# Retention and ELU layer on one core: the second chunk earlier in the opening, and the small weights of two Strassen products moved from GpSimd to VectorE

## Chip, core and metric

The kernel runs on one core of a Trainium2 chip. The metric is the device time of one execution in microseconds. The kernel before takes 636.76 us (median of 3 runs, 635.6 to 637.08). The profiled execution of it has a span of 634.4 us. All data is fp32.

## What is computed

A recurrent retention layer (4 batches, 8 heads, 768 tokens, head size 64) feeds a two-layer network with an ELU between its layers (3072 tokens, width 512, inner width 2048):

```python
for t in range(S):
    state = gamma * state + outer(k[:, :, t], v[:, :, t])
    y[:, :, t] = scale * q[:, :, t] @ state
x = y.transpose(0, 2, 1, 3).reshape(B * S, H * D)       # (3072, 512)
h = x @ w_in                                            # w_in (512, 2048)
g = where(h > 0, h, exp(min(h, 0)) - 1)
out = g @ w_out                                         # w_out (2048, 512)
```

The weights arrive as 64-bit floats, two 32-bit words each, and the kernel turns them into fp32 on the chip.

## The kernel before

**Tiling.** The recurrence is done in chunks of 128 tokens (24 of them), four of which make a block of 512 tokens (6 blocks, called tb 0 to 5). A chunk gets scores (L307), a mask (L318, L328), products for the state after each half of 64 tokens (L338), sums of states (L348, L350), and outputs: products within the chunk (L394) and with earlier states (L409), multiplied by a table of powers of gamma (`etab`, made by ScalarE at L249) into x (L433 for the first two chunks, L384 after that). V is scaled first (L281), by VectorE for chunks 0 and 1 and by GpSimd for the others. Small copies named `seen` stand between two groups of matmuls into the same bank.

**The two GEMMs.** Block 0 has a plain first GEMM (`plain_first`, L489), while the weights are still being decoded. In each piece of weights ScalarE makes three parts (`prepare`, L164 to L168) and VectorE joins them (`decode`, L190 to L194); its `yield`s let the caller place the steps among other work with `take()`. Raw weights and later the small sums pass through the three buffers of the pool `stage`. Block 1 has a Strassen first GEMM with seven products of half size (`first` and `strassen`, L698 to L756, matmuls at L740). Its banks are a (two buffers), b and d (one each). From block 1 on, the second GEMM is Strassen in two levels (`second_twice`, L933): seven outer products, in the order 1, 2, 6, 7, 5, 3, 4, each with seven inner products of four 128-column matmuls at L953. An inner product's sums are L961 and L986 (ScalarE copies) and L965 (VectorE); the inputs of the next outer product are made at L827. From block 2 on, the outer products M2 and M3 of the first GEMM are done in two levels as well (`first_twice`, L865).

**Small weights.** Two-level products need sums of quarters of the weights. They are made once, sent to DRAM (`scratch2` for the second GEMM, `scratch3` for M2 and M3 of the first one), and fetched again in every block into a ring of 11 buffers `wq` (`fetch_small`, L799 and L804), one fetch for each product consumed. For M2 and M3, `combine_small(j)` makes four sums of 128x512 on GpSimd (L816) into a `stage` buffer during the first GEMM of block 1, and puts the transfer on the list `to_send`, which `send_small` issues on the queue of SyncE.

**What sets the order.** The order of every engine's work is written by hand: it is the order of calls in the program, and each engine goes through its own list in order. All DMAs are issued by SyncE, in order too, so that a transfer that waits holds those behind it. Generators are advanced with `next` at chosen places. In the second GEMM of block 1 the generator `sec` yields "first", "middle" and the product's number at each outer product. The caller counts them in `step` (step 1 is outer product 2, step 3 is product 7, step 4 is product 5, step 5 is product 3), and does the recurrence of block 2 at the visits in `VISITS`.

`unread` issues a matmul on a blank tile whose result nobody reads. `hold` copies one element on GpSimd, so that a transfer into a buffer is ordered behind other work.

Of the kernel before, what the change touches and what calls it, by code (L numbers as in the profile page):

```python
# [9 lines left out]
FP32 = mybir.dt.float32  # L10
# [8 lines left out]
def kernel(  # L19
# [32 lines left out]
    nc = tc.nc  # L52
    PSUM = bass.MemoryType.PSUM
    P = nc.NUM_PARTITIONS

    B, H, S, D, DM, DFF = dims
    NTOK = B * S
    C = P
    TB = 512
    TH = TB // 2  # L60
# [51 lines left out]
    def hold(t, other):  # L112

        if other is not None:
            nc.gpsimd.tensor_copy(t[0:1, 0:1], other[0:1, 0:1])
# [28 lines left out]

    def prepare(parts=1, by_vector=False, between=None):

        n = len(prepared)
        if n >= NPIECE:  # L150
            return
        t = staged[n]
        if n < 2 * NQ:
            dst = (w_a, w_b)[n % 2][n // 2].rearrange("p a b c d -> p (a b c d)")
        else:

            dst = w_s[n % NQ].rearrange("p a b c d -> p (a b c d)")[:, 0:1024]
        todo = []
        for part in range(parts):
            if part and between:  # L160
                between()
            c = slice(part * 1024 // parts, (part + 1) * 1024 // parts)
            lo, hi, flat = t[:, c, 0], t[:, c, 1], dst.bitcast(U32)[:, c]
            nc.scalar.activation(flat, lo, AF.Copy, scale=2.0**-29)  # L164
            top = dst.bitcast(F8).rearrange("p (c b) -> p c b", b=4)[:, c, 3]
            nc.scalar.activation(top, hi.bitcast(FP32), AF.Copy, scale=2.0**-120, saturate=False)
            if not by_vector:
                nc.scalar.activation(lo.bitcast(FP32), hi.bitcast(FP32), AF.Copy, scale=2.0**-112)  # L168
            todo.append((lo, flat, hi if by_vector else None))
        prepared.append((dst, todo))  # L170
# [75 lines left out]
    def powers_of(tokens):  # L246
        for a in range(2):
            for u in range(2):
                nc.scalar.activation(etab[:, a, u, tokens], post[:, tokens], AF.Exp, scale=lny[:, a, u : u + 1])  # L249
# [239 lines left out]
    def plain_first():  # L489

        tiles = [(n, w, row, fi) for n in range(NQ) for w, row in ((w_a, 0), (w_b, 1)) for fi in range(2)]
        banks = []

        def part(k, columns):
            n, w, row, fi = tiles[k]
            for j in range(4):
                nc.tensor.matmul(
                    banks[k][:, columns], lhsT=w[n][:, fi, j // 2, j % 2, :], rhs=xb[:, j, columns],
                    start=(j == 0), stop=(j == 3), skip_group_check=True,
                )  # L500

        for k in range(5):
            hp = bank("aabd"[k]) if k < 4 else ps_r.tile([P, 2, TH], FP32, name="hp", tag="r")
            banks.append(hp.rearrange("p a b -> p (a b)"))
            if k == 0:
                part(0, slice(0, C))
                yield
                part(0, slice(C, 2 * C))
            else:
                part(k, half[0])  # L510
            if k:
                yield
        for k in range(5):
            part(k, half[1])
            n, w, row, fi = tiles[k]
            elu(g_plain[row * NF + 2 * n + fi], banks[k])
            yield
        for k, (n, w, row, fi) in enumerate(tiles[5:]):
            hp = bank("aabd"[k % 4]).rearrange("p a b -> p (a b)")
            for j in range(4):  # L520
                nc.tensor.matmul(  # L521
                    hp, lhsT=w[n][:, fi, j // 2, j % 2, :], rhs=xb[:, j, :], start=(j == 0), stop=(j == 3)
                )
            elu(g_plain[row * NF + 2 * n + fi], hp)
            yield
        flush()
# [114 lines left out]
    def send_small():  # L641
        while to_send:
            nc.sync.dma_start(*to_send.pop(0))
# [163 lines left out]

    W_IN = {2: w_a_[:, :, :, 1], 3: w_s_[:, :, 2]}

    def combine_small(j, behind=None):  # L810

        t = stage.tile([P, 4, 4, P], FP32, name="wi", tag="stage")
        hold(t.rearrange("p k f d -> p (k f d)"), behind)
        a11, a12, a21, a22 = (W_IN[j][:, 2 * r : 2 * r + 2, :, c, :] for r in range(2) for c in range(2))
        s1, s2, s3, s4 = (t[:, k].rearrange("p (n f) c -> p n f c", f=2) for k in range(4))
        tt = lambda o, x, y, op: nc.gpsimd.tensor_tensor(out=o, in0=x, in1=y, op=op)  # L816
        tt(s1, a21, a22, ALU.add)
        tt(s2, s1, a11, ALU.subtract)
        tt(s3, a11, a21, ALU.subtract)
        tt(s4, a12, s2, ALU.subtract)  # L820
        to_send.append((scratch3[j - 1], t.rearrange("p k f d -> p (k f d)")))

    xs = {}

# [271 lines left out]
    def take(count=1):  # L1096
        for _ in range(count):
            next(piece, None)
# [3 lines left out]
    def unread(count, n):  # L1102
        for _ in range(count):
            nc.tensor.matmul(warm[:, 0:n], lhsT=blank[:, 0:P], rhs=blank[:, 0:n], start=True, stop=True, skip_group_check=True)
# [15 lines left out]
    y = outputs_of_first()  # L1120
    next(y)
    next(y)
    unread(1, TB)
    score_products(sc, 0, 0, 1)
    state_sum(kvs, 0, 0, 0, 1)
    prepare(2, between=lambda: powers_of(slice(2 * C, S)))
    piece = decode(True)
    take()
    take()
    scale_v(1)  # L1130
    mask_pair(sc, 1)
    inner = plain_first()
    next(inner)
    state_products(kvs, 0, 0, 1, range(2))
    state_sum(kvs, 0, 0, 1, 0)
    next(y)
    next(y)
    next(y)
    unread(1, TB)
    next(y, None)  # L1140
    take()
    take()
# [2 lines left out]
    scale_v(2)  # L1145
    scale_v(3)
    prepare(2, by_vector=True)
    next(inner)
    piece = decode()
    take()  # L1150
    take()
    next(inner)
    scores(0, 1)
    states(0, 1)
# [5 lines left out]
    y = outputs(0, 1)  # L1160
# [115 lines left out]
    sides = [  # L1276
        itertools.chain(combine_w_in(1), last), itertools.chain(combine_w_in(2), combine_w_in(3)), iter(()), iter(()),
    ]
    smalls = [2], [], [3], []
    for n in range(NQ):  # L1280
        load(2 * CPB + n)
        cur = first(n)
        for at in range(3):
            next(cur)

        for _ in tail:
            pass
        for s in cur:
            next(sides[n], None)
            next(sides[n], None)  # L1290
            if s == "gap":
                break
        for _ in sides[n]:
            pass
        tail = cur
        for j in smalls[n]:
            combine_small(j, w_s[1].rearrange("p s a b c -> p (s a b c)") if j == 2 else None)
        send_small()
    for m in range(2 * CPB, 3 * CPB):
        scale_v(m)  # L1300
# [14 lines left out]
        pass  # L1315
    flush()
    step, VISITS = 0, [(0, "end"), (2, "middle"), (3, "first"), (4, "end"), (5, "end")]
    for s in sec:
        if s == "first":
            step += 1  # L1320
        at = (step, s if s in ("first", "middle") else "end")
        if at in VISITS:
            retention_step(2, VISITS.index(at))
        if s == ORDER2[-1]:
            break
    tail = sec
# [150 lines left out]
```

## Time and profile before

| part of the page | value |
|---|---|
| span | 634.4 us |
| TensorE busy | 626.7 us, 99% |
| VectorE busy | 481.7 us, 76% |
| ScalarE busy | 252.9 us, 40% |
| GpSimd busy | 40.6 us, 6% |
| DMA | 136.85 MB, mean 216 GB/s |

The page and the timeline call TensorE's matmuls PE, its weight loads PEld, VectorE DVE, ScalarE ACT, GpSimd POOL, and SyncE's queue SPq. A line of the timeline has the start in us from the span's start, the duration in us, engine, line of the program, operation, and what it writes and reads with shapes and count; in brackets stands the engine's idle time just before it, with the work whose end released it. The ends of matmuls are modelled: a group's listed duration is about 0.16 us longer than its share of TensorE, so the steps between starts are the better measure. The steps are 0.893 us for an inner product at L953, 1.73 us for a product at L740 or at L497 with 256 columns.

The opening lasts until about 30 us. The first GEMM of block 1 runs from 135 to 186 us, the second GEMM of block 1 from 182 to about 240.

### The profile page before, as it was taken

The page shows a single profiled execution, that of the slowest core. Times are in us where ns is not written, and L with a number is a line of the kernel's source. Part 1 is how long each engine was busy: PE and PEld are TensorE (multiplying, and loading weights), DVE is VectorE, ACT ScalarE, POOL GpSimd, SP SyncE. Part 2 cuts the span into 40 slices and gives each one's busy share as a digit, 9 for nine tenths or more (in the row PEclk, how much of TensorE's full clock was granted, in tenths as well). Part 3 has the DMA queues.
Part 4 walks back from the last instruction along what each step waited for, and adds up shares of the span by engine and source line. Part 5 has one row for each costly group of instructions (what it writes and reads, how often), then busy time and mean ns, then how long its engine had stood idle before and what let it go on. Part 6 is the DMA issues. An engine that isn't in the chain of part 4 may idle for free.

```text
span 634.4 us, 16149 instructions
## 1 busy us (share of the span) xinstructions
PE 626.7 (99%) x6680; PEld 560.7 (88%) x6680; DVE 481.7 (76%) x870; ACT 252.9 (40%) x472; POOL 40.6 (6%) x40
## 2 busy tenths in 40 slices
PE   8999999999999999999999999999999999999998
PEld 5764568888899999889999989999988999988997
DVE  5779979978879685589676598867489878558975
ACT  6599635014551113554112556111465311366311
POOL 1111000003600000200000100000110000000000
PEclk9999999999999999999999999999999999999999
DMA  8698867687477778504889701789820697700794
GB/s 336 264 390 307 269 205 222 189 248 258 176 239 228 242 254 272 239 2 135 277 267 312 290 4 55 258 283 286 302 100 4 218 299 236 238 24 2 231 309 158
DMA packets 75897, 136.85 MB, mean 216 GB/s; under 512 B 6320, under 2 KB 31792, under 8 KB 70704
## 3 DMA queue, kind: packets, MB, share of 16 engines
q1 hardware_dynamic: 75824, 135.82, 64.2%
q8 instruction: 53, 0.87, 0.5%
q14 instruction: 20, 0.16, 0.1%
HBM read 114.56 MB, written 21.23 MB: 214 GB/s over the span
## 4 chain that ended last, share of the span: by engine, by line
PE 94%; DVE 4%; issue 1%; ACT 0%; DVEq 0%
PE pa L953 20%; PE pa L911 10%; PE pd L953 10%; PE pb L953 5%; PE pa L865 5%; PE pb L911 4%; PE pa L521 3%; PE qa L911 3%; PE x L611 3%; PE pa L740 2%; PE pd L865 2%; PE qd L911 2%; PE pd L911 2%; PE pa L611 2%; PE y L394 2%; PE kv L338 2%
## 5 line engine op out<-in xcount | busy, mean ns | idle before, releaser
L961 ACT COPY ms<-pa 128x128 f32<-128x128 f32 x104 | 27.6, 265 | 147.1 <-PE pa L953 143.7
L953 PE MATMUL pa<-ts,wq 128*128 128x128 f32 x560 | 74.2, 275 | 0.0
L953 PE MATMUL pd<-ts,wq 128*128 128x128 f32 x552 | 73.6, 276 | 0.1
L953 PEld LDWEIGHTS pa<-ts,wq 128*128 128x128 f32 x560 | 68.5, 192 | 0.4
L953 PEld LDWEIGHTS pd<-ts,wq 128*128 128x128 f32 x552 | 67.1, 192 | 0.9 <-DVE res L965 0.5
L953 PE MATMUL pa<-gC,wq 128*128 128x128 f32 x480 | 64.6, 278 | 0.0
L478 ACT ACTIVATE r<-r 128x512 f32<-128x512 f32 x96 | 60.5, 631 | 3.0
L953 PEld LDWEIGHTS pa<-gC,wq 128*128 128x128 f32 x480 | 59.0, 192 | 1.3
L477 ACT ACTIVATE r<-gC 128x512 f32<-128x512 f32 x64 | 39.9, 624 | 32.0 <-DVE gC L919 32.0
L965 DVE TENSOR_TENSOR res<-pd,ms 128x128 f32<-128x128 f32 x68 | 19.4, 286 | 39.6 <-PE pd L953 38.4
L281 POOL TENSOR_TENSOR chunk<-chunk,vf 128x512 f32<-128x512 f32 x22 | 26.3, 1199 | 318.4 <-DMA chunk<-in_qkv_dram 153.5
L481 DVE SCALAR_TENSOR_TENSOR gC<-r,gC 128x512 f32<-128x512 f32 x64 | 44.3, 724 | 0.7 <-ACT r L478 0.7
L827 DVE TENSOR_TENSOR ts<-gC,ts 128x512 f32<-128x512 f32 x60 | 41.3, 688 | 1.0
L827 DVE TENSOR_TENSOR ts<-gC 128x512 f32<-128x512 f32 x60 | 40.9, 682 | 0.0
L953 PE MATMUL pb<-gC,wq 128*128 128x128 f32 x240 | 31.7, 275 | 0.0
L986 ACT COPY res<-pa 128x128 f32<-128x128 f32 x34 | 9.0, 265 | 55.1 <-PE pa L953 55.1
L953 PEld LDWEIGHTS pb<-gC,wq 128*128 128x128 f32 x240 | 29.2, 192 | 0.0
L690 ACT COPY m<-pa 128x512 f32<-128x512 f32 x24 | 13.9, 581 | 30.1 <-PE pa L911 14.2
L919 DVE TENSOR_TENSOR gC<-qa,gC 128x512 f32<-128x512 f32 x8 | 5.5, 692 | 25.1 <-PE qa L911 18.3
L911 PE MATMUL pa<-xt,w_s 128*128 128x256 f32 x96 | 23.0, 382 | 0.0
L911 PE MATMUL pa<-xt,w_b 128*128 128x256 f32 x96 | 23.0, 382 | 0.0
L965 DVE TENSOR_TENSOR res<-res 128x512 f32<-128x512 f32 (+1 forms) x31 | 20.6, 666 | 3.0 <-DVE res L965 0.5
(256 smaller groups left out, 1258.4 us busy)
## 6 DMA issues: line engine op xcount, KB each, us to landing
wq<-scratch_dram SPq DMA_DIRECT2D x277, 256.0 KB, 4.2
chunk<-in_qkv_dram SPq DMA_DIRECT2D x23, 1024.0 KB, 8.3
wraw<-in_w_dram SPq DMA_DIRECT2D x15, 1024.0 KB, 6.1
out_dram<-res SPq DMA_DIRECT2D x14, 256.0 KB, 3.8
scratch_dram<-gT SPq DMA_DIRECT2D x12, 256.0 KB, 4.2
scratch_dram<-m SPq DMA_DIRECT2D x12, 192.0 KB, 5.6
scratch_dram<-so SPq DMA_DIRECT2D x4, 512.0 KB, 4.8
scratch_dram<-wi SPq DMA_DIRECT2D x2, 1024.0 KB, 5.1
```

What stands on the lines that cost most here:

```text
L281: eng.tensor_tensor(out=kv[:, 1], in0=kv[:, 1], in1=vf[:, i].unsqueeze(2).to_broadcast([C, H, D]), op=ALU.mult)
L477: nc.scalar.activation(e, h, AF.Relu, scale=-1.0)
L478: nc.scalar.activation(e, e, AF.Exp, scale=-1.0)
L481: nc.vector.scalar_tensor_tensor(g, e, -1.0, h, ALU.add, ALU.max)
L521: nc.tensor.matmul(hp, lhsT=w[n][:, fi, j // 2, j % 2, :], rhs=xb[:, j, :], start=(j == 0), stop=(j == 3))
L611: nc.tensor.matmul(X[j][:, d, :], lhsT=w[j][:, d * P : d * P + P], rhs=x[j], start=(n == 0 and d == 0), stop=at_end, skip_group_check=True,)
L827: sub = lambda o, x, y: nc.vector.tensor_tensor(out=o, in0=x, in1=y, op=ALU.subtract)
L865: nc.tensor.matmul(ps[:, f, :], lhsT=lhs[f], rhs=xs[j][k], start=(begin and f == 0), stop=True, skip_group_check=True,)
L911: nc.tensor.matmul(ps[:, fi, :], lhsT=w[:, fi, j2, :], rhs=x[:, j2, :], start=(j in (1, 7) and fi == 0 and j2 == 0), stop=(j2 == 1), skip_ ...
L953: nc.tensor.matmul(ps, lhsT=w[:, f, :], rhs=ts[j][k][:, f, :], start=(begin and f == 0), stop=(f == 3), skip_group_check=True,)
L961: nc.scalar.copy(m, ps)
L965: nc.vector.tensor_tensor(out=o, in0=x, in1=y, op=ALU.add)
```

## The change

It has two parts.

In the opening, the work of chunk 1 (scores, scaling, mask, states, outputs) goes ahead of the decode of the first weights and of the first columns of the first GEMM, which used to stand between its scores and its state products. One blank matmul becomes half as wide, and one is dropped. ScalarE makes the powers for tokens 256 and up (L249) after the weights' first two pieces, and no longer between the halves of the first. The tile k = 3 of `plain_first` is done in two halves of columns, with the scores and states of chunks 2 and 3 between them.

The eight small sums of M2 and M3 leave GpSimd and the first GEMM of block 1. VectorE makes them in the second GEMM of block 1, in four pairs, at the visits listed in `SUMS`. They go into the buffer `xt`, which lies idle there, and M2's and M3's sums use it one after the other: M3's first sum overwrites what M2's transfer reads. The transfers are issued at the end of step 3 and in the middle of step 5.

```diff
-    def prepare(parts=1, by_vector=False, between=None):
+    def prepare(parts=1, by_vector=False):
...
-            if part and between:
-                between()
...
+            elif k == 3:
+                part(k, slice(0, C))
+                yield
+                part(k, slice(C, 2 * C))
...
-    def combine_small(j, behind=None):
+    def combine_small(j):
-        t = stage.tile([P, 4, 4, P], FP32, name="wi", tag="stage")
-        hold(t.rearrange("p k f d -> p (k f d)"), behind)
+        t = xt_.rearrange("p j a (b c) -> p j (a b) c", c=P)
...
-        tt = lambda o, x, y, op: nc.gpsimd.tensor_tensor(out=o, in0=x, in1=y, op=op)
+        tt = lambda o, x, y, op: nc.vector.tensor_tensor(out=o, in0=x, in1=y, op=op)
         tt(s1, a21, a22, ALU.add)
         tt(s2, s1, a11, ALU.subtract)
+        yield
         tt(s3, a11, a21, ALU.subtract)
         tt(s4, a12, s2, ALU.subtract)
         to_send.append((scratch3[j - 1], t.rearrange("p k f d -> p (k f d)")))
+        yield
...
-    unread(1, TB)
+    unread(1, TH)
     score_products(sc, 0, 0, 1)
     state_sum(kvs, 0, 0, 0, 1)
-    prepare(2, between=lambda: powers_of(slice(2 * C, S)))
+    prepare(2)
     piece = decode(True)
-    take()
-    take()
     scale_v(1)
     mask_pair(sc, 1)
-    inner = plain_first()
-    next(inner)
     state_products(kvs, 0, 0, 1, range(2))
     state_sum(kvs, 0, 0, 1, 0)
     next(y)
+    take()
     next(y)
+    take()
     next(y)
-    unread(1, TB)
+    inner = plain_first()
+    next(inner)
     next(y, None)
...
     prepare(2, by_vector=True)
+    powers_of(slice(2 * C, S))
     next(inner)
     piece = decode()
     take()
     take()
+    next(inner)
     next(inner)
     scores(0, 1)
...
-    smalls = [2], [], [3], []
...
-        for j in smalls[n]:
-            combine_small(j, w_s[1].rearrange("p s a b c -> p (s a b c)") if j == 2 else None)
         send_small()
...
+    smalls = itertools.chain(combine_small(2), combine_small(3))
+    SUMS = [(3, "first"), (3, "middle"), (4, "end"), (5, "first")]
     for s in sec:
...
+        if at in SUMS:
+            next(smalls)
+        if at in ((3, "end"), (5, "middle")):
+            send_small()
```

## The prediction

> **What bounds the kernel now.** TensorE does. I read the page's shares first (PE 99% of a 634.4 us span), then its slices, then TensorE's own timeline, for the few places where it waits.
>
> ```profile
> PE   8999999999999999999999999999999999999998
> ...
> PEclk9999999999999999999999999999999999999999
> ```
>
> Only the first and last slices of PE fall below 9, and the granted clock is full throughout. So the change can win only what TensorE waits in two places, and can lose wherever it makes TensorE wait anew. The first place is the opening:
>
> ```profile
> 10.81 0.69 PE L307 MATMUL sc<-chunk 64*64 64x64 f32 x32
> 11.83 1.13 PE L497 MATMUL pa<-xb,w_a 128*128 128x128 f32 x8 [0.33 <-DVE w_a L194]
> 12.89 0.69 PE L338 MATMUL kv<-chunk 64*64 64x64 f32 x32
> ...
> 15.20 1.12 PE L1104 MATMUL pa<-blank 128*128 128x512 f32 x2
> 16.16 3.11 PE L497 MATMUL pa<-xb,w_a 128*128 128x128 f32 x16
> 19.79 1.99 PE L497 MATMUL pb<-xb,w_b 128*128 128x256 f32 x8 [0.52 <-DVE w_b L194]
> ```
>
> Chunk 1 has landed by 10.8, but its state products (L338) begin at 12.89, since the decode of w_a and the first GEMM columns go first. The 512-column product on blank at 15.20 is filler. The second place is the first GEMM of block 1, with PE, DVE and POOL side by side:
>
> ```profile
> 153.56 1.99 PE L740 MATMUL pd<-xb,w_s 128*128 128x256 f32 x8 [0.73 <-DVE h L695]
> ...
> 166.42 1.99 PE L740 MATMUL pd<-xb,w_s 128*128 128x256 f32 x8 [0.44 <-DVE h L695]
> ```
> ```profile
> 146.14 1.63 DVE L647 TENSOR_TENSOR wi<-w_s 128x384 f32<-128x384 f32 x1
> 147.81 1.51 DVE L647 TENSOR_TENSOR wi<-wi,w_s 128x384 f32<-128x384 f32 x1
> 149.24 0.54 DVE L647 TENSOR_TENSOR wi<-w_s 128x384 f32<-128x384 f32 x1
> ```
> ```profile
> 145.63 1.73 POOL L816 TENSOR_TENSOR wi<-w_a 128x512 f32<-128x512 f32 x1
> ```
>
> The same VectorE sum takes 0.54 us alone and 1.5 to 1.6 us beside GpSimd's; VectorE then is late with the L695 sum that frees bank d, and TensorE waits.
>
> [...] The trace agrees (0.54 against 1.63 above; the L695 sums, with one input in PSUM, stay at 0.69 beside a busy GpSimd). [...] No wait here is over 0.8 us and the clock is full[...]. [...]
>
> **Part 1, the opening.** Chunk 1's work moves ahead of the w_a decode, the columns 0:128 of tile 0 behind it; one filler is halved (its end is hidden by chunk 1's landing, cost and gain nothing), one is gone, the 2.55 us of powers (L249) move into ScalarE's idle 17.7 to 22.9 (nothing), and tile 3 is split around the scores. Walked with the durations of the timeline: V scaled 10.8 to 11.5 (0.68), masks to 12.2 (0.75), state sum 12.25 to 12.7, within-chunk products to 12.8, across-chunk to 13.4, the `seen` copies to 13.7 (the decode step is emitted behind them and ends at 14.3), remaining across-chunk to 14.2, the two outputs (L433) 14.25 to 15.0. They began at 15.34: 1.1 us earlier. Columns 0:128 then run 14.35 to 15.25 and 128:256 to 16.1. The second half of w_a needs ScalarE, which is tied to its DMA (about 12.3) and is done by 14.4; its decode runs to 16.1, tile 1 from 16.15 to 17.9. The decode of w_b's first half was L194 at 18.43, stretched to 1.31 us by GpSimd's scale of chunk 2 at 18.12 (landing-bound, stays). It now runs 17.3 to 18.0, ahead of that scale, so tile 2 starts at 18.05, not 19.79: 1.7. The second half then meets the scale, ends at about 20.2, and tile 3's first half waits 0.45 for it. Scores 21.15, states 22.15, rest of tile 3 23.2, outputs of pair 1 at 24.1 for 25.66: **1.55 us** remain. After 28.5 TensorE waits for nothing until 153, so this should reach the end. Ends: 0.6 (if bound to DMA landings) and 1.9.
>
> **Part 2, removed from GpSimd.** Eight L816 sums (1.27 to 1.73 us each) and a 1x1 copy go. From 142.30 to 157.18 TensorE needed 14.88 us for eight products of 1.73 plus one gap's worth: 8 x 1.7265 = 13.81, so 1.07 lost; from 157.18 to 170.05 seven products are 12.09 of 12.87, so 0.78 lost. Sum 1.85 us. Something comes back: the loads of chunks 9 to 11 stood behind the small sends on the queue and their scales behind the sums (POOL 168 to 176.6). Now they load at about 148.5 and are scaled at about 153 to 160, where VectorE has no idle. Each scale (1.04 us) delays a two-SBUF-input operation by about 0.6 (L481 at 175.82: 1.30 for 0.68), 1.8 in all, against about 1.6 of slack which I count ahead of the L695 sum of the second wait (VectorE's 11.2 us of work from 151.2 end at 162.4, it may end at 164.0). I take 0.2 lost: **gain 1.65**; ends 1.15 and 1.85.
>
> **Part 3, added to VectorE.** Eight 128x512 sums in pairs. A pair costs what a pair of L827 costs: 0.71 + 0.61 = 1.32. They write the idle xt tile: last read by L740 in block 1's first GEMM (186), next written by L454 at 241.67. Where they fall:
>
> ```profile
> 215.65 0.29 DVE L965 TENSOR_TENSOR res<-pd,ms 128x128 f32<-128x128 f32 x1 [0.41 <-ACT ms L961]
> ...
> 234.71 0.28 DVE L965 TENSOR_TENSOR res<-pd,ms 128x128 f32<-128x128 f32 x1
> ```
> ```profile
> 217.83 1.06 PE L953 MATMUL pd<-ts,wq 128*128 128x128 f32 x8
> ...
> 235.16 1.06 PE L953 MATMUL pd<-ts,wq 128*128 128x128 f32 x8
> ```
>
> The first two pairs stand on each side of four L827 sums, ahead of the 215.65 add. That add moves to 212.63 + 1.32 + 2.6 + 1.2 = 217.7 and ends at 218.0; the product into bank d, due at 217.83, waits for it: 0.2, with its restart 0.3. The third pair lands in VectorE's idle 1.43 before the add at 226.93: nothing, if the first send has landed (issued about 218, 5.1 us for 1 MB by the DMA list, against the pair's 224.9). The fourth pair costs in full: from 226.93 to 237.2 VectorE has no idle at all, and the add at 234.71 ends 0.17 before TensorE writes bank d at 235.16. So +1.32 there, on top of the 0.3: **cost 1.6 us**. The next block, without added sums, shows how tight that point is:
>
> ```profile
> 335.36 0.28 DVE L965 TENSOR_TENSOR res<-pd,ms 128x128 f32<-128x128 f32 x1
> ```
> ```profile
> 335.70 1.16 PE L953 MATMUL pd<-ts,wq 128*128 128x128 f32 x8
> ```
>
> There the add comes 0.80 after the start of the product before it (334.56), in block 1 only 0.44 (234.27): 0.36 later, and the chain of waits already runs through it. Ends of the cost: 0.3 and 2.6. The sends (SyncE) delay weight fetches behind them: the first by 2 us (weights come 10 us ahead, landing 4.2), the second holds the first fetch for M3 until about 237; it lands at 242, its product comes at about 248. Nothing.
>
> **Sum**: -1.55 - 1.65 + 1.6 = -1.6, so 636.76 becomes **635.1 us**.
>
> **The rivals.** *VectorE absorbs the sums* (18%): the fourth pair is made up because TensorE's finish, not VectorE, starts each run; cost 0.3, gains 1.55 + 1.85: -3.1, 633.7. For it: VectorE is only 64 to 74% busy there; against it: the 0.17. *The gains are smaller* (20%): the opening is held by landings (0.6), the chunk scales keep 0.7 of the middle waits (1.15), cost 1.6: -0.15, 636.6. For it: DMA at 0.92 to 1.03 share from 5 to 25 us. *A new wait on xt* (12%, slower): the third pair overwrites the tile that the first send still reads; with 8.3 us to landing, as 1 MB chunk loads take, the pair waits from 224.9 to 226.3, its 0.7 of slack goes and 0.7 is added, and the fifth stage starts later by a restart, 0.3: cost 2.6; with no gain in the opening and 1.15 in the middle: +1.45, 638.2. For it: VectorE is in order; against it: the 5.1 measured for sends of this size.
>
> **Numbers.** The forecast has 50%. Around it the error is some 0.6 us, so 36 of these 50 are faster by over 0.2% (1.27 us), 14 within. With the absorbing case (18) and 3 of the second rival: faster 57%, same 31%, slower 12%. The range 633.6 to 637.0 holds the absorbing case and the small-gain one and leaves out the new wait.
>
> **What would show it.** Right: outputs of pair 1 at about 24.1; no L740 wait of over 0.3 us between 140 and 170; from about 209 to 235 TensorE falls back by about 1.6, most of it at the bank-d product of the last inner stage, released by the L965 add. Wrong: that product not waiting (cost too high), a wait of L817 for a DMA on xt (the slow rival), or an opening that gains under 1 us (landings).

## The result and the profile after

The changed kernel takes **640.73 us** (median of 4 runs, 639.2 to 641.51) against 636.67 (4 runs) of the kernel before: ratio 1.006, 95% interval 1.0037 to 1.0084. The forecast was 635.1, with 637.0 as the upper end of its range: it has the wrong sign, and none of its rivals reaches so high. The profiled executions span 639.0 us (after) and 634.4 us (before), a difference of 4.5 us.

First the page of the kernel after, part 2, the slices of TensorE and of its granted clock:

```profile
PE   7899999999999989999999999999999999999998
...
PEclk9999999999999999999999999999999999999999
```

Two slices more than before have fallen below 9: the one from 16 to 32 us, in the opening, and the one from about 224 to 240 us, in the second GEMM of block 1; the first slice has gone from 8 to 7. The clock is still full. So the loss is again in places where TensorE waits, and the list of its waits names them (columns: who waits, for whom; us in total, how often, the longest):

```profile
PE pb L956 <- issue: 2.1, 1, 2.1
...
PE pd L495 <- DVE w_b L192: 1.3, 1, 1.3
PE pd L742 <- DVE h L697: 0.7, 1, 0.7
PE pd L956 <- DVE res L968: 0.7, 1, 0.7
PE kv L336 <- issue: 0.7, 1, 0.7
PE y L407 <- issue: 0.6, 1, 0.6
```

Three of the six shown are put down to "issue": the profile shows nothing that TensorE waited for. They sum to 3.4 us, and the prediction had no term for any of them.

To see where the time goes, I took the start of the first product of five stages from TensorE's timeline, for every kernel that ran, and subtracted neighbours (us). "To hp" is the opening up to the first product of the fifth tile of the first GEMM of block 0; the next columns end at the first GEMM of block 1, at its second GEMM, and at the first GEMM of block 2 (its products with 128 columns).

```
kernel                        to hp  to 1st GEMM   1st GEMM   2nd GEMM   rest   span
                                     of block 1    block 1    block 1
before                        28.50    106.90       46.74      58.32    393.98  634.4
before, profiled again        28.00    106.78       46.74      58.33    393.99  633.8
after                         29.80    107.41       45.98      62.14    393.64  639.0
e1  opening alone             29.35    106.43       46.72      59.01    394.49  636.0
e9  opening, no split         30.36    107.36       46.72      58.33    393.65  636.4
e3  after, no split           27.43    107.40       45.87      61.34    393.65  635.7
e11 after, V scaled by DVE    29.36    106.95       45.86      63.44    394.37  640.0
e2  sums alone                28.01    107.36       46.08      61.28    393.64  636.4
e5  after, no sums            29.59    106.41       45.83      59.82    393.63  635.3
e4  after, sends early        29.87    107.35       44.90      60.49    393.63  636.2
e10 after, half sends         29.31    107.14       45.84      63.78    393.58  639.6
e6  after, less filler        31.23    107.86       45.83      65.90    394.36  645.2
e7  sums in idle places       29.30    106.65       46.04      58.87    395.33  636.2
e8  all together              27.13    106.44       44.89      59.04    397.77  635.3
```

After minus before: +1.30, +0.51, -0.76, +3.82, -0.34, in all +4.53. The opening, meant to win 1.55, lost 1.3; the first GEMM of block 1 won half of what was forecast; its second GEMM, expected to give up 1.6, gave up 3.8. (The second column lies between 106.4 and 107.9. e2, whose instructions are those of before up to the end of that stretch, has 107.36, so I put the 0.5 down to neither part. The 0.34 of the last column is not explained.)

The opening on TensorE, kernel after (start, duration, line, tiles, count, and in brackets the idle time before it with its releaser):

```profile
14.84 3.77 PE L495 MATMUL pa<-xb,w_a 128*128 128x128 f32 x24 [0.23 <-ACT wraw L166]
18.62 1.97 PE L495 MATMUL pb<-xb,w_b 128*128 128x256 f32 x8
21.91 1.16 PE L495 MATMUL pd<-xb,w_b 128*128 128x128 f32 x8 [1.32 <-DVE w_b L192]
23.00 1.16 PE L305 MATMUL sc<-chunk 64*64 64x64 f32 x64
...
28.36 0.69 PE L407 MATMUL y<-chunk 64*64 64x64 f32 x31 [0.33 <-DVE seen L376]
29.66 0.21 PE L407 MATMUL y<-chunk 64*64 64x64 f32 x1 [0.61 <-issue]
29.80 1.56 PE L495 MATMUL hp<-xb,w_a 128*128 128x256 f32 x6
```

Up to tile 2 most of the forecast gain is there: tile 2 starts at 18.62, for 18.05 forecast and 19.79 before. Then tile 3's first half, now ahead of the scores, stands 1.32 us on the second half of w_b, and everything behind it in TensorE's order stands too. VectorE and GpSimd at that moment:

```profile
18.39 1.29 DVE L188 TENSOR_SCALAR wraw<-wraw 128x512 f32<-128x512 f32 x1
...
20.28 1.57 DVE L192 CUSTOM_DVE_ANT_0 w_b<-wraw,w_b 128x1024 uint16<-128x1024 uint16 x1
```
```profile
17.80 1.58 POOL L279 TENSOR_TENSOR chunk<-chunk,vf 128x512 f32<-128x512 f32 x1 [2.40 <-DVE wraw L189]
20.27 1.04 POOL L279 TENSOR_TENSOR chunk<-chunk,vf 128x512 f32<-128x512 f32 x1 [0.89 <-DMA chunk<-in_qkv_dram]
```

Not one but two steps of the decode fall beside GpSimd's scales of V: 1.29 us for a step that takes 0.42 alone, and 1.57 for one of 0.69. The decode ends at 21.85; the forecast had 20.2. (The second scale was there before as well, at 20.37, beside a decode step that began at 20.67 and took 1.31 us; the forecast counted one scale alone.)

The second GEMM of block 1, TensorE and then VectorE:

```profile
225.40 0.50 PE L956 MATMUL pb<-gC,wq 128*128 128x128 f32 x3
227.97 0.82 PE L956 MATMUL pb<-gC,wq 128*128 128x128 f32 x5 [2.07 <-issue]
...
239.93 1.16 PE L956 MATMUL pd<-ts,wq 128*128 128x128 f32 x8 [0.73 <-DVE res L968]
```
```profile
239.60 0.28 DVE L968 TENSOR_TENSOR res<-pd,ms 128x128 f32<-128x128 f32 x1
```

The wait of 0.73 is the one foreseen for the fourth pair of sums, behind the add of bank d. That of 2.07 is new: it falls in the middle of a product, between the third and the fourth of eight recorded matmuls with the same input, the same weight tile and the same bank (each matmul of the program leaves two records here: eight for the four of an inner product). The profile shows no semaphore that the fourth waited for.

**What "issue" was here.** The trace records, beside the data transfers, a queue of packets of 16,384 bytes that carry instructions:

```profile
q8 instruction: 53, 0.87, 0.5%
```

There are 53 of them in each of eight profiles (before twice, after, e6, e8 to e11), for some 13,400 recorded matmuls and weight loads of TensorE, so one for about 126 matmuls; I read them as TensorE's own instructions. One of them lies from 225.70 to 226.63; TensorE goes on at 227.97, 1.34 us after it has landed. In the kernel after, four of the 53 have a wait put down to issue of 0.2 us or more behind them (2.07, 0.70, 0.61 and 0.23 us), in the kernel before none. The theory that the experiments test is that TensorE stands when such a packet comes late; the rival is that the wait belongs to the work at that place.

### The profile page after: what moved, and what is told of

It reads as the page before. It is cut to its first block, busy times and chain, and to the rows that moved or that the text cites. A ratio compares the mean times of both kernels' runs of the same rounds, so it can differ in the third digit from the quotient of the medians.

```text
span 639.0 us, 16160 instructions
## 1 busy us (share of the span) xinstructions
PE 625.2 (98%) x6686; PEld 560.6 (88%) x6686; DVE 483.4 (76%) x878; ACT 252.8 (40%) x472; POOL 27.1 (4%) x31
## 4 chain that ended last, share of the span: by engine, by line
PE 86%; DVE 8%; issue 2%; ACT 1%; DMA 1%; SPq 0%; DVEq 0%
PE pa L956 19%; PE pa L914 10%; PE pd L956 10%; PE pb L956 5%; PE pa L868 5%; PE pb L914 4%; PE qa L914 3%; PE x L613 3%; PE pa L742 3%; PE pd L868 2%; PE qd L914 2%; PE pd L914 2%; PE pa L613 2%; PE y L392 2%; PE pd L742 2%
## 5 line engine op out<-in xcount | busy, mean ns | idle before, releaser
L956 PEld LDWEIGHTS pb<-gC,wq 128*128 128x128 f32 x240 | 29.3, 192 | 2.3 <-issue 2.3
L914 PE MATMUL pa<-xb,w_a 128*128 128x256 f32 x96 | 22.7, 379 | 0.0
```

Source lines behind the costliest of these rows:

```text
L914: nc.tensor.matmul(ps[:, fi, :], lhsT=w[:, fi, j2, :], rhs=x[:, j2, :], start=(j in (1, 7) and fi == 0 and j2 == 0), stop=(j2 == 1), skip_ ...
L956: nc.tensor.matmul(ps, lhsT=w[:, f, :], rhs=ts[j][k][:, f, :], start=(begin and f == 0), stop=(f == 3), skip_group_check=True,)
```

## The experiments

All ratios are to the kernel before, run on the same chip, with 95% intervals.

**The opening alone (e1)** and **the sums alone (e2).** Each is the kernel before with one half of the diff.

```diff
 # e1: before, with the new order of the opening and
+            elif k == 3:
+                part(k, slice(0, C))
+                yield
+                part(k, slice(C, 2 * C))
 # e2: before, with the sums of combine_small on nc.vector into xt, and
+    SUMS = [(3, "first"), (3, "middle"), (4, "end"), (5, "first")]
```

> The opening's part alone; the small sums stay on GpSimd. Theory A (the opening loses, because the first half of tile 3 now waits for w_b's decode ahead of the scores, and because TensorE sits in the middle of groups with no semaphore to wait for): the product after the first GEMM's fifth tile starts about 1.1 us later than before, the time is 1.1 to 1.9 us over before (ratio 1.002 to 1.003). Theory B (the prediction's: the opening gains and the loss is all in the second GEMM): 1.5 us under before (ratio 0.9976). The two waits of L740 for VectorE, 0.73 and 0.44 us, stay in both.

> The small sums' part alone, with the opening as before. Theory A (the send of 1 MB holds up TensorE's instruction stream, a stall of about 2 us in the middle of an inner product in the fourth or fifth outer product, beside 1.3 us of VectorE's queue and 0.8 to 1.2 us saved in the first GEMM): 2 to 2.5 us over before (ratio 1.003 to 1.004). Theory B (the sums cost only VectorE's queue): within 0.5 us of before (ratio 0.999 to 1.001), with no stall in the middle of a product.

Measured: e1 1.003 (1.0016 to 1.0045), e2 1.0022 (1.0008 to 1.0035). Each half makes the kernel slower by itself. The opening of e1 ends at 29.35, within the 29.3 to 29.9 of every kernel with the split and the full filler; e2, with the opening of before, at 28.01. What the second GEMM of block 1 loses belongs mostly to the sums' half: +2.96 in e2 (1.2 of it a wait put down to issue), +0.69 in e1.

**The sends moved (e4)** and **the sums left out (e5).** e4 is the kernel after with the two sends of xt made in the first GEMM of block 1 (they carry what xt holds then, not the sums). e5 is the kernel after with the eight additions left out; xt is sent as it is.

```diff
 # e4, in the loop of the first GEMM of block 1
+        for j in ([2], [], [3], [])[n]:
+            to_send.append((scratch3[j - 1], xt_.rearrange("p j a t -> p (j a t)")))
 # e5
-        tt(s1, a21, a22, ALU.add)
-        tt(s2, s1, a11, ALU.subtract)
...
-        tt(s3, a11, a21, ALU.subtract)
-        tt(s4, a12, s2, ALU.subtract)
```

> The changed kernel with its two 1 MB sends issued during the first GEMM of block 1, where the kernel before had them; they then carry what xt held before the sums, so the small weights of M2 and M3 are left out of the result. The sums stay where the change put them. Theory A (the send holds up TensorE's instructions or weights): the 2.07 us stall in the middle of the product into bank b is gone, and the time is about 2 us under the changed kernel (ratio to before about 1.003). Theory B (VectorE's sums hold TensorE there, by whatever path): the stall stays, ratio 1.006. The wait of the bank-d product of the last inner stage, 0.73 us in the changed kernel, stays in both and grows.

> The changed kernel with the eight sums left out, so that the two sends, in their places, carry what xt held. Theory A (stall by the send; 1.3 us by VectorE's queue, apart from each other): the stall of about 2 us in the middle of a product stays, the waits of bank-d products for L968 vanish, about 1.3 us under the changed kernel (ratio to before about 1.004). Theory B (VectorE's sums are behind all of it): no stall, about 3.4 us under the changed kernel (ratio 1.001).

Measured: e4 1.0022 (0.9999 to 1.0044), e5 1.0027 (1.0012 to 1.0043). TensorE's waits from 140 us (e4) and 183 us (e5) to 245 us:

```profile
PE pd L955 <- DVE res L967: 0.7, 1, 0.7
PE pb L955 <- issue: 0.4, 1, 0.4
```
```profile
PE pb L952 <- issue: 1.2, 1, 1.2
```

The two losses come apart. Without sends at that place the wait for instructions falls from 2.07 to 0.4 and the wait for the bank-d add stays; without sums the bank-d wait goes and 1.2 of the other stays. (That last figure is no measure of the sums' share: e2 and e3, with the same sums and sends, have 1.2 and 1.4.) e4 also shows something that I hadn't asked of it: no wait is left in the first GEMM of block 1, which takes 44.90 us, 1.84 less than before. Its sends stand ahead of the loads of chunks 9 to 11 in the queue, and the last of GpSimd's scales runs at 167.34 instead of 162.29 us.

**Less filler (e6).** 12 filler matmuls of 64x64 instead of 28: each later matmul stands 16 places earlier in the program, which is 32 recorded matmuls (6654 in all for 6686). The expectation below took 16 places of the program for 16 recorded rows.

```diff
-    for n in range(28):
+    for n in range(12):
```

> The kernel after, with 12 filler matmuls of 64x64 in the opening instead of 28, so that every later matmul stands 16 places earlier in TensorE's instruction stream. If the wait of 2.07 us in the second GEMM of block 1 is one for the next block of instructions, it stays at the same row of the stream (2377) and so falls 16 matmuls further on in the work: at 230 to 231 us, in the bank-d product L956 after the one where it was, not in the bank-b product at 227.97; its length may change, since the sends are then further behind it. If it belongs to the work (the product, its weights, the bank), it stays in the bank-b product with its 2 us. Time between 638.5 and 641 either way; the opening's waits put down to issue should move by 16 matmuls as well.

Measured: 1.0162 (1.0125 to 1.0198), far outside what I had expected. But its profile is the clearest on the cause. The opening, and the second GEMM of block 1:

```profile
13.26 0.27 PE L392 MATMUL pb<-chunk 64*64 64x64 f32 x2 [0.71 <-issue]
...
28.68 0.70 PE L392 MATMUL y<-chunk 64*64 64x64 f32 x33 [2.76 <-issue]
...
211.33 1.33 PE L336 MATMUL kv<-chunk 64*64 64x64 f32 x24 [2.89 <-issue]
...
233.22 1.06 PE L956 MATMUL pb<-gC,wq 128*128 128x128 f32 x8
```

Counting TensorE's recorded matmuls from 0, the first wait in the opening stands before row 223 in both kernels. In the kernel after that is a state product (L336), here it is an output product (L392). The wait of 2.76 stands before row 477: in e1 and e11 (below) that matmul belongs to tile 3, here to the outputs. The bank-b product that stood for 2.07 us runs through. So the waits stay with positions in the stream and not with the work: the expectation of the instruction theory. Its other half, that the wait at row 2377 moves on in the work, can't be seen here; that block was in time, and one three blocks earlier (211 us) was late. e2 and e3 show it. They have six and eight recorded matmuls fewer ahead of that place, and they wait at the same row, to within one, which now lies in the next product, the one into bank a. In e3:

```profile
223.81 0.39 PE L952 MATMUL pa<-gC,wq 128*128 128x128 f32 x2
225.56 0.83 PE L952 MATMUL pa<-gC,wq 128*128 128x128 f32 x6 [1.36 <-issue]
```

The size of e6's loss has a second part: after each of the two long waits the granted clock was down.

```profile
30.00:36.00 6.00, 5.83 (x49) 5.04 (x50) 3.04 (x7) 0.51 (x1) 0.00 (x0) 0.72 0.21 46
...
212.00:218.00 6.00, 6.00 (x39) 5.88 (x36) 1.56 (x4) 0.53 (x2) 0.00 (x0) 0.52 0.26 65
```

(Busy time of PE, PEld, DVE, ACT and POOL in each stretch, then clock, DMA share, GB/s.) Behind the waits of 2.76 and 2.89 us the mean clock was 0.72 from 30 to 36 us and 0.52 from 212 to 218; elsewhere it fell behind shorter waits (below).

**Smaller sends (e10).** The kernel after with each 1 MB send made as two of 512 KB at different times.

```diff
-        if at in ((3, "end"), (5, "middle")):
+        if at in ((3, "middle"), (4, "first"), (5, "first"), (5, "middle")):
             send_small()
```

> The kernel after, with each of the two 1 MB sends made as two of 512 KB at different times (about 217.5, 221.5, 233 and 237 us); the sums stay where they were. If the 2.07 us wait of the bank-b product at 227.97 comes from the megabyte in front of TensorE's next block of instructions, it falls below 1 us, and block 1's second GEMM loses about 2.5 us against the kernel before instead of 3.8: 639.5 us. If the size of a send does not matter, the wait stays at 1.5 to 2.1 us and the time at 640.7. The wait of 0.7 us behind the bank-d add is to stay in both.

Measured: 1.0047 (1.0033 to 1.0062). The wait is the same to the matmul:

```profile
224.50 0.50 PE L958 MATMUL pb<-gC,wq 128*128 128x128 f32 x3
227.07 0.84 PE L958 MATMUL pb<-gC,wq 128*128 128x128 f32 x5 [2.07 <-issue]
```

So my picture of one megabyte in front of the instructions was wrong: the halves, issued at 215.18 and 219.80, do as much harm. The DMA engines were no freer: share 1.05 from 220 to 222 us and 1.03 from 224 to 226, as after (1.07 and 0.99), where the kernel before had 0.84 and 0.52. (Its second GEMM takes 63.78 us, more than the 62.14 of the kernel after: from 227.8 to 231.1 its granted clock was 0.50.)

What goes with the wait in all kernels is how late the packet starts. I took the moment at which row 2250 starts (a few records are missing, so the row is good to some matmuls), one block before the wait, and the start of the next instruction packet:

```
kernel         packet starts after row 2250    wait put down to issue there
e9                       2.3 us                      0
before (twice)           2.6, 2.6                    0
e6, e7, e8               2.9, 2.9, 3.0               0
e1, e4                   3.4, 3.6                    0.5, 0.4
e3, e2, e5               4.2, 4.3, 4.4               1.4, 1.2, 1.2
e11, after, e10          5.1, 5.2, 5.2               2.0, 2.1, 2.1
```

The block's matmuls take 5.2 us when nothing stands (from 219.84 to 225.05 in the kernel before). The packet takes 0.9 (0.93 in the kernel after) and TensorE goes on about 1.3 us after it has landed (1.34), so it may start about 3 us after the row (an estimate: 5.2 less 0.9 and 1.3); each microsecond beyond has about a microsecond of waiting beside it in the table (3.4 and 0.5, 5.2 and 2.1). The six kernels at the bottom all issue a send of xt in the 5 us or so before that row. That isn't enough for a late packet, though: e6, e7 and e8 do so too and don't wait. e7 issues its halves at 215.17 and 221.43 us, 5.0 before the row and 1.3 after it, with a DMA share of 1.02 from 220 to 222 us and 1.03 from 224 to 226, and its packet is in time.

**The split of tile 3.** e3 is the kernel after with tile 3 in one piece behind scores and states; e9 is e1 without the split; e11 keeps the split, but takes away what made it wait: VectorE scales chunks 2 and 3 itself, behind the decode of w_b.

```diff
 # e3 and e9
-            elif k == 3:
-                part(k, slice(0, C))
-                yield
-                part(k, slice(C, 2 * C))
...
-    next(inner)
 # e11
-        eng = nc.vector if m < 2 else nc.gpsimd
+        eng = nc.vector if m < 4 else nc.gpsimd
...
-    scale_v(2)
-    scale_v(3)
     prepare(2, by_vector=True)
...
     take()
     take()
+    scale_v(2)
+    scale_v(3)
```

> The kernel after, with tile 3 again done in one piece behind the scores and states (its first 128 columns no longer ahead of them). If the split is what the opening loses by (tile 3's first half waits 1.32 us in TensorE's order for the second half of w_b), pair 1's scores begin at about 21.0 instead of 23.0 and the opening is 1.2 us shorter than in the kernel after: near 639.5 us, and the shift against the kernel before at 31 us is about 0. If the opening loses by TensorE's instruction blocks[...], the waits put down to issue take the place of the one that is gone and the shift at 31 us stays near +1: 640.5. Everything behind 31 us should be as in the kernel after: the 2 us wait put down to issue at row 2377 of TensorE's matmuls stays.

> The new order of the opening alone (chunk 1 first, half the filler, the powers later), without the split of tile 3; the sums on GpSimd as in the kernel before. If the split is what turned the opening's gain into a loss, the fifth tile's first product (hp) begins at about 27.4 us, as in the kernel after without the split, against 28.5 before and 29.4 to 29.9 with it: a gain of 0.5 to 1.1 us, 635.7 to 636.3 us, ratio 0.999. If the opening's time is set by when loads and instruction blocks land, which differ from run to run, hp begins anywhere between 28 and 29.5, and the ratio is 1.000 to 1.003 as with the split.

> The kernel after with the split of tile 3 kept, but the two scales of chunks 2 and 3 (1.58 and 1.04 us on GpSimd, beside the decode of w_b) done by VectorE behind that decode, so that nothing stretches it: the second half of w_b should be decoded by 20.1 us instead of 21.85, and tile 3's first half should wait under 0.3 us instead of 1.32. If the stretched decode is all that the split loses by, the fifth tile's first product (hp) begins at about 28.3 instead of 29.8, and the time falls by 1.3 to 1.5 us: ratio about 1.0035 to the kernel before for 1.006. If the split also loses by waits put down to issue that come with it (rows 477 and 605 of TensorE's matmuls in five of the six profiles with the split, none in the profiles without), these stay at 0.5 to 1.2 us each, hp begins at 29 to 29.5, and the ratio stays at 1.005 or more.

Measured: e3 1.0008 (0.9989 to 1.0028) where the kernel after has 1.006; e9 0.9989 (0.9974 to 1.0003) where e1, the same with the split, has 1.003. Both pairs say that the split costs 0.4 to 0.5%, some 2.6 to 3.3 us, and that the rest of the new opening order costs nothing or gains a little. (e9's own profile isn't a good witness of it: there a wait of 1.6 us for instructions ended at 13.28, and from 14 to 21 us the granted clock was 0.51.) One cost of the new order stays without the split: in all ten kernels that have it TensorE stood for 0.3 to 1.6 us before row 223, in the four profiles with the old order not at all. e3's opening:

```profile
20.41 1.16 PE L305 MATMUL sc<-chunk 64*64 64x64 f32 x64
21.39 1.11 PE L336 MATMUL kv<-chunk 64*64 64x64 f32 x64
22.43 1.99 PE L495 MATMUL pd<-xb,w_b 128*128 128x256 f32 x8
...
27.43 0.89 PE L495 MATMUL hp<-xb,w_a 128*128 128x256 f32 x3
```

The scores run while w_b is still being decoded, and hp comes 1.07 us earlier than before. e11 shows that the split costs more than its own wait. Its ratio is 1.0058 (1.0037 to 1.0079), no better than after, though the wait for w_b is gone:

```profile
20.14 1.05 PE L495 MATMUL pd<-xb,w_b 128*128 128x128 f32 x8
21.12 1.16 PE L305 MATMUL sc<-chunk 64*64 64x64 f32 x64
22.10 1.11 PE L336 MATMUL kv<-chunk 64*64 64x64 f32 x64
23.14 1.05 PE L495 MATMUL pd<-xb,w_b 128*128 128x128 f32 x7
25.77 0.27 PE L495 MATMUL pd<-xb,w_b 128*128 128x128 f32 x1 [1.57 <-issue]
...
29.22 0.21 PE L407 MATMUL y<-chunk 64*64 64x64 f32 x1 [0.61 <-issue]
29.36 1.99 PE L495 MATMUL hp<-xb,w_a 128*128 128x256 f32 x8
```

Scores at 21.12, states at 22.10, the rest of tile 3 at 23.14: the times of my walk (21.15, 22.15, 23.2), now that the decode ends at 19.8. And then TensorE stands, once on its last matmul of tile 3 and once on the last of the outputs, for the blocks whose packets start at 23.40 and 26.89 us. Taking one wait away, 1.32 us, brought hp forward by 0.44. In the profiles with the split, one or both of these two block ends (rows 477 and 605) stood for 0.5 to 2.8 us; in those without it there was no wait of more than 0.2 us at them. In the kernel after, 127 of the 128 recorded matmuls between the two ends are products of 64x64, which TensorE runs at about 15 ns each (64 from 21.12 to 22.10 in e11); this block took 3.45 us in most kernels with the split, which is 1.1 from its beginning to the next packet's start, 1.0 for the packet and 1.3 to go on. Tile 3 in halves has eight recorded matmuls more than in one piece, so that the block begins and ends eight places earlier in the work. In e3 the same rows hold 121 products of 64x64 and seven matmuls of hp with 256 columns (0.22 us each), which fill the time until the next block is there. That these slow matmuls are what is missed is my reading; that the waits come with the split is what the runs show.

**The sums at idle places (e7).** The opening of before; each pair of sums directly ahead of an add that waits for TensorE anyway, and each pair sent on its own.

```diff
             if j == 1:
                 yield "tail"
+            if at in (2, 3, 4, 5) and tb == 1:
+                yield "idle"
             for _ in before:
...
     for s in sec:
+        if s == "idle":
+            next(smalls)
+            continue
...
-        if at in SUMS:
-            next(smalls)
-        if at in ((3, "end"), (5, "middle")):
+        if at in ((2, "first"), (3, "middle"), (4, "middle"), (5, "middle")):
```

> The opening of the kernel before, the eight sums on VectorE as in the kernel after, but each pair at a place where VectorE waits for TensorE anyway (directly ahead of the add that reads bank d of the inner stage before, in the second to fifth inner stages; idle there 0.63, 1.22, 1.43 and 1.43 us in the kernel before, for pairs of 1.32), and each pair sent on its own, 512 KB, at four different times. If the cost of the sums was their place in VectorE's queue and that of the sends the backlog in front of TensorE's instruction blocks, the gain in the first GEMM of block 1 (0.8 to 1.1 us) stays and at most 0.5 comes back: 635.7 to 636.3 us, ratio 0.999. If VectorE or the sends cost the same wherever they stand, it is as the sums alone were: 638 to 638.6.

Measured: 0.9997 (0.9977 to 1.0018), against 1.0022 for the same sums in the change's places. From 183 to 245 us no wait of TensorE is left, and the second GEMM of block 1 costs 0.55 us over before instead of 2.96. The sends differ from e2's too, so only the end of the bank-d wait (0.7 in e2) is the places' own; the wait for instructions (1.2 in e2) may be gone by the sends or by chance. VectorE's lines show how the place works: the third pair takes the gap ahead of the bank-d add, which follows at 219.23.

```profile
217.51 0.29 DVE L968 TENSOR_TENSOR res<-pb,ms 128x128 f32<-128x128 f32 x1 [1.27 <-PE pb L956]
217.72 0.68 DVE L815 TENSOR_TENSOR xt<-w_s 128x512 f32<-128x512 f32 x1
218.44 0.69 DVE L815 TENSOR_TENSOR xt<-xt,w_s 128x512 f32<-128x512 f32 x1
```

In its profiled run a block came late in block 2 instead (1.5 us at 303), and the opening waited 1.0 for a chunk's landing, so that the span, 636.2, doesn't show the gain.

**All together (e8)**: the new opening without the split, the sums of e7, and the loads of chunks 10 and 11 held by the last sum on w_s (the way in which the kernel before held a buffer), so that GpSimd's scales come later (their last ends at 167.4 us, for 163.6 in the kernel after).

```diff
 # e3 and e7, and
-        load(2 * CPB + n)
+        load(2 * CPB + n, behind=w_s[3].rearrange("p s a b c -> p (s a b c)") if n > 1 else None)
```

> What the runs so far point to, together: the new order of the opening without the split; the eight sums on VectorE at the places where it waits for TensorE anyway, each pair sent as 512 KB; and the loads of chunks 10 and 11 held until the last small weights of the first GEMM are summed (162 us), so that GpSimd's scales of them come later, where the run with the early sends had no wait left in the first GEMM of block 1. If the three causes are the ones named: opening -0.5 to -1.1, first GEMM of block 1 -0.8 to -1.7, sums +0.5: 634.5 to 636 us, ratio 0.997 to 0.999. If waits for instruction blocks set the time whatever is moved, they appear elsewhere, and it is 636.5 to 638.

Measured: 635.85 us against 636.54, ratio **0.9978 (0.9964 to 0.9993)**, the only kernel of the study that is faster than before by more than its interval. Opening 27.13, first GEMM of block 1 44.89, no wait of TensorE between 130 and 245 us: at the end of the second GEMM of block 1 it stands 2.96 us ahead of before. Then in the profiled run:

```profile
PE y L408 <- issue: 2.4, 1, 2.4
```
```profile
300.00:304.00 4.00, 1.81 (x13) 1.75 (x13) 1.67 (x6) 0.00 (x0) 0.00 (x0) 0.82 0.40 146
304.00:308.00 4.00, 4.00 (x30) 4.00 (x29) 0.33 (x2) 0.53 (x2) 0.00 (x0) 0.75 0.38 100
```

One late block, with the clock drop behind it, takes 3.8 us back (rest 397.77 for 393.98). The runs of e8 spread from 633.2 to 639.14 us.

**Before, profiled again (b2).**

> The kernel before once more, to see how much of the opening and of the waits put down to issue differs between two runs of one kernel. If the opening is set by TensorE's order and VectorE's work, hp begins within 0.2 us of the 28.50 of the first profile; if landings and instruction blocks set it, it may differ by 0.5 to 1 us, and waits put down to issue stand at other rows.

Its opening ended at 28.00 and its span was 633.8; it has no wait put down to issue, and its two waits in the first GEMM of block 1 are there again. So two profiles of one kernel differ by half a microsecond in the opening, and e7, with the same opening, ended at 29.30. A single opening can't be read closer than that; the ratios above can.

## Why the prediction was wrong

**The opening, -1.55: became +1.3.** The walk held in its order up to tile 2, with 1.17 us won for 1.7. The step that failed first is "ends at about 20.2, and tile 3's first half waits 0.45 for it": the decode met two scales and not one, ended at 21.85, and the wait was 1.32. (The prediction counts the delay for an operation with two SBUF inputs; the stretched step L188, 1.29 us for 0.42, reads one tile.) The step that failed worse is the next one, "Scores 21.15, states 22.15, rest of tile 3 23.2, outputs of pair 1 at 24.1". e11 made its times true to within 0.1 us and won nothing in the whole time: the walk took for granted that TensorE always has its next instruction, and there it hadn't. The second rival gave this part a smaller gain, bound by landings of data; instructions weren't thought of. (The prediction's "No wait here is over 0.8 us" also leaves out a wait of 1.5 us for the blank tile at the very start, which the change doesn't touch. That halving one blank matmul and dropping another costs nothing was an estimate: no run changes these alone.) Without the split the new order reached 27.13 and 27.43 in e8 and e3, 1.1 to 1.4 less than before's 28.50 and 0.6 to 0.9 less than its 28.00, but 30.36 in e9 with its early wait. So a part of the forecast gain may be there; e9's ratio, whose interval includes 1, doesn't show it clear of the noise.

**The removal from GpSimd, -1.65: became -0.76.** The wait at 153.56 is gone; the one at 166.42 stayed, as

```profile
167.47 1.99 PE L742 MATMUL pd<-xb,w_s 128*128 128x256 f32 x8 [0.74 <-DVE h L697]
```

The mechanism was right, and the term "I take 0.2 lost" was mis-sized: the scales, now at 157 to 163 us, kept a wait of 0.74 and cost 1.1 of the 1.85. So the slack of 1.6 us that I set against them didn't cover them; the second rival's "the chunk scales keep 0.7 of the middle waits" is what happened. e4 and e8, in which these scales come later and GpSimd's sums are gone as well, took 44.90 and 44.89: the full 1.85.

**The sums on VectorE, +1.6: right, 1.3 measured.** From 183 to 219 us TensorE fell back by 0.2 to 0.3, for "0.3"; at 239.93 by 1.0 (the wait of 0.73 and its restart: 3.77 us behind before at 237.15 and 4.77 at 239.93), for 1.32. The product and the releaser are those named, and no sum waited for a send. What was wrong was the word behind it: for **the sends** the prediction says "Nothing", having asked only what stands behind them on SyncE's queue. That is the step that failed in this stage. Around the sends TensorE stood the 2.07 us for its instructions, 2.3 with the restart (it was 1.35 us behind before at 225.40 and 3.69 at 228.63); with the sends moved away (e4) 0.42 was left. Sum of the parts: +1.3 + 0.5 - 0.8 + 1.5 (with 0.2 more of small shifts) + 2.3 - 0.3 = 4.5.

**Open:** why a packet comes late. The sends take part in it (e4), but neither a send nearby nor a DMA share near 1.0 is enough, as e7 shows. Whether the packet stands behind data packets on the DMA engines or is asked for late, no run separates.

## What to carry to other kernels

A wait put down to issue between two matmuls of one product is a place to look for the engine's own instruction packets in the trace. Moving the sends into another GEMM left 0.42 us of 2.07 (e4); halving them within the same GEMM left all of it in one kernel (e10) and nothing in two others (e7, e8). As these waits stayed with positions in the stream, a change far ahead of them moved them onto other work (six and eight recorded matmuls fewer put the wait at row 2377 into the next product in e2 and e3), and each kernel has to be looked at anew. Work added to VectorE, a quarter idle here, was free of a wait only where it stood at the idle moment: the same eight sums held TensorE behind the bank-d add for 0.7 us in one order (e2) and not at all in another (e7). And a product put ahead of others "because its half is ready" has to be checked against when it is ready: tile 3's first half stood 1.32 us, and the scores behind it in TensorE's order began at 23.00 us, where e3, with the scores first, had them at 20.41.

## What the runs showed of the hardware

- The packets of the instruction queue have 16,384 bytes and mostly take 0.9 to 1.1 us (46 of the 53 in the kernel after; its longest takes 1.68). A block of 127 matmuls of 64x64 and one other, rows 477 to 605, took 3.45 us in the kernel after; at the 15 ns each of an undisturbed group they would take about 2 (an estimate from 64 in 0.98 us in e11).
- TensorE resumed 1.2 to 1.6 us after such a packet had landed, in all waits put down to issue of over 0.25 us (1.51, 1.21 and 1.34 us in the kernel after).
- These waits stood at the same recorded rows in several kernels (223, 477, 605 and 2377, counted from 0 and to within one), with different work there (at 223 a state product, L336, in the kernel after and an output product, L392, in e6).
- The mean granted clock was 0.50 over 3.0 to 3.3 us behind waits of 2.0 to 2.8 us (e11, e10, e8, e6), 0.50 over 6.5 us behind one of 2.9 (e6), and 0.51 over 7 us in an opening with a wait of 1.6 (e9). It stayed at 1.00 after the 2.07 of the kernel after.
- SyncE's queue ran in order: in the kernel before a send waited 15.0 us in it for GpSimd's sums (L816), and the chunk load behind it was issued at 168.53 us, 0.37 after the send. So did TensorE's list: the scores behind tile 3's first half began at 23.00 us (after), ahead of it at 20.41 (e3).
- One VectorE operation beside GpSimd's, in the kernel after: 1.29 us for 0.42 (L188, which reads one tile) and 1.57 for 0.69 (L192).
